# Gated linear attention and a channel mixer on one core: even-odd token order, column pieces of a weight, and a new issue order

## The chip, the core and the metric

The program runs on one core of a Trainium2 chip. The core has a matrix engine (TensorE, PE in the profile; its weight loads are PEld), VectorE (DVE), ScalarE (ACT), GpSimd (POOL) and SyncE (SP), which here only issues transfers. Sixteen DMA engines move data between HBM, the large memory, and SBUF, the memory on the chip; matmuls write into PSUM, eight banks of 2 KB per partition. The metric is the device time of one execution in microseconds (us), the median of several runs.

## The reference

Inputs are q, k, v and alpha of shape (4, 8, 768, 48), float32, and four weight matrices. First a recurrent attention for each batch and head, then a mixer over tokens and over channels:

```python
state = zeros(B, H, D, D)
for t in range(S):
    state = alpha[:, :, t, :, None] * state + einsum('bhd,bhe->bhde', k[:, :, t], v[:, :, t])
    y[:, :, t] = einsum('bhd,bhde->bhe', q[:, :, t], state)
x = y, as (B, 768, 384)
u = x + (relu(x^T @ w_tok1) @ w_tok2)^T          # w_tok1 768x256, w_tok2 256x768
out = u + relu(u @ w_ch1) @ w_ch2                # w_ch1 384x1536, w_ch2 1536x384
```

## The kernel before

The recurrence is computed in chunks of 256 tokens: three chunks per batch, n = 0 to 11. A partition of an input tile holds two neighbouring tokens (slots 0 and 1) of all 8 heads; the 128 partitions make two halves of 64, hf = 0 and 1, each with its own 128 tokens, and the state is carried from half to half. For one chunk the steps are: load alpha (`ld_at`), k, q, v; logarithms of alpha on ACT (`ln`, `lnP`); cumulative sums by a triangular matmul (`cum`, `cumw`); exponentials `E` and `IE` on ACT; k and q scaled by them (`kk`, `qq`); transposes of both. Chunks 0 to 5 transpose on TensorE into a PSUM bank (`trk`, `trq`), copied out by `evk` and `evq` into tiles tpk and tpq; chunks 6 to 11 transpose by a DMA issued on SP (`dk`, `dq`), and the query's result is copied once more (`pq`) into tpq. Then scores `G0`, `G1` for the two halves, a triangular mask on DVE (`mask`, tile gtm), the outer products `K`, the state updates `sa`, `sm`, `s`, the outputs `ia`, `ib`, `y`, and their copy to bf16 `x0`, `x1`.

The mixer of batch b takes the six x tiles of 128 tokens: `t1` (token matmul 1, six steps for each of two output blocks), `ht` (its relu), `t2` (token matmul 2) and `u` (the sum, on DVE). u is transposed to channels first: batch 0 on TensorE (`up`, `ut`), batches 1 to 3 by DMA on SP (`ux`). Then `c1`, 12 blocks of 128 channels for each half of the tokens, with relu `rt`; `c2`, 12 accumulating steps in four groups for each of six token tiles; the output sum `o` on DVE into one of three tiles o; and the store `st`, 192 KB, to HBM. The last batch's tile 0 is done in two half-wide parts (h0, h1).

Weights are loaded as 384 KB pieces into the pool of 19 input tiles (`ldw_`) and cast to bf16 (`cw_`): w_tok1 (wt1) and w_tok2 (wt2) in two pieces each, w_ch1 (wc1) and w_ch2 (wc2) in six each. In this kernel a piece of wc1 is 128 rows by 768 columns, so a `c1` block waits for three pieces.

The order of the work is written out: the text `ORDER` lists every operation in one sequence with a letter for its engine (t PE, s ACT, v DVE, g POOL, y SP), and `BUFS` the buffer of every tile. Each engine runs its operations in this order and waits at each for what it needs, so an operation that waits holds back all that follow on its engine. The entry `f8_trk0` and its like are fillers: matmuls on a zero tile ahead of the named operation, 8 units of 512 columns; every three units are issued as one float32 matmul (two rows in the profile), the rest as bf16. Operations on DVE and POOL that use the port which both share are also ordered one after another.

In the tiles tpq and tpk the 128 tokens of one half lie side by side. What comes from the transposes has the two slots apart, so the copies put them together. Before, the query copies place the two slots alternately, token by token:

```python
def qev(self, e, d, s):
    self.copy(e, self.t(d).rearrange("p (j c s) -> p s j c", j=4, s=2),
              s.rearrange("p (s j c) -> p s j c", s=2, j=4))
```

and the key copies place them as runs of 64 (slot 0, then slot 1, within each half).

Of the kernel before, what the change touches and what calls it, by code (L numbers as in the profile page):

```python
# [9 lines left out]
BF16 = mybir.dt.bfloat16  # L10
AF = mybir.ActivationFunctionType
ALU = mybir.AluOpType
# [89 lines left out]
UP = (0,)  # L102
# [11 lines left out]
SLOT = ()  # L114
# [6 lines left out]
def build(g):  # L121
# [18 lines left out]
    def attention(n):  # L140
# [64 lines left out]
        if n in KX:  # L205
            evk = O("dk", {"SP": (1240.0, 1240.0)}, 9, writes=[tpk], reads=[pkk], preds=kk,
                    emit=lambda e: g.xbar(tpk, pkk), dma=("x", 1400.0, 1180.0, 480.0))
            k_read = evk
        else:
            bk = V("one")  # L210
            k_read = O("trk", pe([128] * 8), 8, writes=[bk], reads=[pkk], preds=kk,
                       emit=lambda e: g.trw(bk, pkk))
            evk = O("evk", either(dve(1024, True), act(1024)), 9, writes=[tpk], reads=[bk], preds=[k_read],
                    emit=lambda e: g.trwev(e, tpk, bk, n not in SLOT))
        if n in QX:
# [3 lines left out]
            evq = O("pq", either(dve(1024), act(1024 * 1.35, True), {"POOL": (1100.0, 1140.0)}), 9.5, port=True, writes=[tpq], reads=[tqx], preds=[xq],  # L219
                    emit=lambda e: g.qev(e, tpq, g.t(tqx)))  # L220
        else:
# [3 lines left out]
            evq = O("evq", either(dve(1024 * 1.065), act(1024 * 1.34)), 9, writes=[tpq], reads=[bq], preds=[trq],  # L225
                    emit=lambda e: g.qev(e, tpq, g.bank(bq).bitcast(BF16)))
# [82 lines left out]
    def weight(nm, piece, prio, work=1100.0):  # L309
        raw = V("in")  # L310
        o = P.op(f"ldw_{nm}{piece}", LOADQ[0], prio, writes=[raw],
                 emit=lambda e: g.weight(e, nm, piece, raw, o), dma=("i", work, 1500.0, 650.0))
        wl[(nm, piece)] = P.op(f"cw_{nm}{piece}", either(dve(768, nm != "wc1"), pool_cp(768), act(768, True)), prio + 1,
                               reads=[raw], preds=[o], port=True, emit=lambda e: g.wcast(e, nm, piece, raw))

    def mixer(b):
# [16 lines left out]
        for i in range(NS):  # L333
            if i % 3 == 0:
# [3 lines left out]
                     reads=[h for h, _ in hts], preds=[h for _, h in hts] + [wl[("wt2", p)] for p in range(2)],  # L338
# [71 lines left out]
ld_at1y ld_at0y ln1s ln0s f8_cumw1t f1_cumw1t cumw1t IE1s cumw0t IE0s ld_vt0y E0s vb0g vs0_0g vs1_0v ld_kt0y kk0v  # L410
f8_trk0t f1_trk0t trk0t E1s ld_qt0y qq0v ka0s kb0s kc0v f1_trq0t trq0t ld_kt1y kk1v K0t evq0s s0_0v ld_vt1y vb1s
f1_trk1t trk1t ld_at2y evk0v ln2s f2_G0_0t G0_0t ld_qt1y ka1g sa1_0v f4_cumw2t cumw2t mask0_0v vs0_1s kb1g kc1g vs1_1s
K1t sm1_0g qq1v sa0_1v sm0_1v G1_0t ld_kt2y IE2s E2s trq1t evq1s ib0t mask1_0v f3_y1_0t y1_0t y0_0t evk1v G0_1t sa1_1v
ld_qt2y x1_0s mask0_1v G1_1t ld_vt2y x0_0s vb2s kk2g trk2t kc2s ldw_wt10y qq2g cw_wt10s f2_ia1t ia1t mask1_1v evk2s
trq2t ld_at3y vs1_2g ldw_wt11y evq2v ib1t y1_1t y0_1t vs0_2g ldw_wt21y sm1_1g P3g K2t sa0_2v sm0_2g x0_1s t1_0_0_0t
f1_G0_2t G0_2t ldw_wt20y G1_2t cw_wt20g t1_0_1_0t mask0_2v x1_1s t1_0_1_1t ld_at4y ld_kt3y t1_0_1_2t lnP3s cum3t
cw_wt11s IE3s ia2t y0_2t x0_2s t1_0_0_1t t1_0_0_2t E3s t1_0_0_3t mask1_2v t1_0_1_3t ib2t y1_2t ldw_wc14y t1_0_1_4t
x1_2s t1_0_0_4t f1_t1_0_1_5t t1_0_1_5t ht_0_1v P4g cw_wt21s t1_0_0_5t ht_0_0s f3_t2_0_0t t2_0_0t t2_0_1t u_0_0v ln13s
r13s ldw_wc13y t2_0_2t u_0_1v t2_0_3t u_0_2v t2_0_5t lnP4s t2_0_4t u_0_3v u_0_5v u_0_4v up_0_0t cw_wc14s cw_wc13s
ldw_wc15y up_0_1t ld_qt3y k0a3g kk3g cum4t trk3t cw_wc15g ut_0_0v up_0_2t ut_0_2v ut_0_1s c1_0_11_0t c1_0_8_0t IE4s  # L420
c1_0_11_1t rt_0_8_0v rt_0_11_0v ldw_wc11y q0r3g qq3g c1_0_9_1t rt_0_9_1v ln14s kb3s c1_0_10_0t cw_wc11s c1_0_9_0t
rt_0_9_0v rt_0_11_1v E4s c1_0_7_0t c1_0_10_1t c1_0_7_1t ldw_wc10y r14s cw_wc10s rt_0_10_1v trq3t evk3s rt_0_7_0v
ldw_wc12y ld_vt3y cw_wc12g c1_0_2_0t c1_0_0_1t ka3g rt_0_7_1s c1_0_8_1t rt_0_10_0v vb3v vs1_3g vs0_3g rt_0_0_1v
rt_0_2_0v evq3s ld_at5y ld_qt4y c1_0_1_1t rt_0_8_1v c1_0_3_0t kc3s K3t P5g c1_0_4_1t rt_0_3_0s rt_0_1_1s q0r4g G0_3t
ld_kt4y qq4g s0_3v ln15s G1_3t sa1_3v c1_0_2_1t rt_0_2_1s mask0_3v lnP5s c1_0_1_0t c1_0_5_1t rt_0_5_1s rt_0_1_0s r15s
mask1_3v ldw_wc21y cw_wc21s k0a4g ldw_wc20y c1_0_6_1t rt_0_6_1v c1_0_4_0t kk4v ldw_wc22y c1_0_5_0t c1_0_0_0t cw_wc22s
rt_0_4_0v rt_0_0_0v cw_wc20g rt_0_4_1s c1_0_6_0t rt_0_6_0v c1_0_3_1t trq4t rt_0_3_1v cum5t trk4t ld_kt5y k0a5g
ldw_wc23y rt_0_5_0s c2_0_3_0t c2_0_5_0t evq4s kb4s evk4v ld_qt5y G1_4t mask1_4v G0_4t ld_vt4y c2_0_0_0t IE5s c2_0_0_1t
ka4g cw_wc23s c2_0_3_1t kc4s sm1_3g E5s mask0_4v ib3t y1_3t ldw_wc24y cw_wc24s c2_0_5_1t vb4g vs1_4s x1_3s ia4t
ldw_wc25y vs0_4g cw_wc25s ld_at6y y0_3t kk5v c2_0_3_2t y0_4t q0r5v trk5t evk5s qq5v K4t c2_0_0_2t sa0_4v c2_0_0_3t P6v  # L430
x0_3s ld_at7y sm0_4g o_0_0v trq5t x0_4s sa1_4v P7g evq5s lnP6s c2_0_5_2t c2_0_5_3t ld_vt5y vb5g c2_0_4_0t c2_0_4_1t
ld_kt7y kc5g G1_5t G0_5t lnP7s o_0_5v ib4t y1_4t vs1_5s mask1_5v t1_1_1_0t t1_1_1_1t sm1_4g x1_4s c2_0_4_2t c2_0_3_3t
vs0_5s ld_at8y t1_1_1_2t st_0_5s K5t mask0_5v sa0_5v sm0_5v cum6t t1_1_0_0t ld_kt6y k0a6g t1_1_0_1t ld_qt6y c2_0_2_0t
ln17s ld_qt7y ia5t y0_5t x0_5s IE6s kk6g ib5t y1_5t ln16s E6s t1_1_0_2t x1_5v t1_1_0_3t t1_1_1_3t cum7t E7s o_0_3v
t1_1_1_4t t1_1_1_5t r16s ld_kt8y q0r6g ld_vt6y dk6y P8g ht_1_1v lnP8s t1_1_0_4t t1_1_0_5t c2_0_2_1t c2_0_2_2t ln18s
ht_1_0v t2_1_1t u_1_1v t2_1_2t t2_1_0t t2_1_4t u_1_2v u_1_0v ux_1_0y c2_0_1_0t c2_0_1_1t vb6s IE7s qq6v r17s t2_1_3t
u_1_3v c2_0_2_3t ka6s kc6s t2_1_5t o_0_2v u_1_4v c2_0_1_2t st_0_0y st_0_3s cum8t k0a8g c2_0_1_3t u_1_5v q0r7v vs1_6v
dq6y c2_0_4_3t c1_1_8_0t rt_1_8_0v IE8s c1_1_11_0t vs0_6s c1_1_5_0t E8s c1_1_10_0t o_0_4v c1_1_4_0t k0a7g ux_1_1y
o_0_1v kb6g rt_1_4_0v pq6s K6t s0_6v sa1_6v c1_1_3_0t rt_1_3_0v c1_1_0_0t rt_1_5_0s ld_at9y rt_1_0_0v rt_1_11_0s
c1_1_10_1t c1_1_2_0t c1_1_6_0t rt_1_6_0v r18s G0_6t G1_6t rt_1_10_0s rt_1_10_1s c1_1_1_0t qq7g rt_1_2_0s mask1_6v  # L440
c1_1_7_0t rt_1_7_0v ld_vt7y ld_qt8y c1_1_6_1t rt_1_6_1v c1_1_9_1t c1_1_11_1t kk7g ka7s vb7s c1_1_8_1t st_0_1s ld_at10y
kk8g rt_1_1_0s mask0_6v c1_1_3_1t ib6t rt_1_9_1v rt_1_3_1v c1_1_1_1t rt_1_8_1s P9g y0_6t vs1_7s x0_6v q0r8g c1_1_7_1t
qq8g rt_1_7_1v rt_1_11_1s y1_6t c1_1_5_1t rt_1_5_1v dk8y rt_1_1_1s vs0_7v dq7y kb7v sm1_6v c1_1_9_0t dk7y kc7g
c2_1_2_0t c1_1_2_1t rt_1_9_0v c1_1_0_1t lnP9s cum9t E9s x1_6v c2_1_2_1t c1_1_4_1t rt_1_4_1v pq7g K7t IE9s c2_1_2_2t
c2_1_2_3t sa0_7v rt_1_2_1s st_0_2y dq8y pq8g ld_vt8y G1_7t G0_7t mask1_7v ld_at11y sm0_7g sa1_7v ld_qt9y rt_1_0_1s
# [520 lines left out]
```

## Time and profile before

| | |
|---|---|
| timed runs | 163.34, 163.48, 164.39 us; median 163.48 |
| profiled execution | span of 160.5 us from the first to the last instruction; the profile gives no other time of it |
| median less span | 3.0 us |
| PE, PEld busy | 154.6 us (96%), 97.1 us (60%) |
| DVE, ACT, POOL busy | 114.9, 97.8, 80.8 us |
| DMA | 35.05 MB in 76,130 packets; 25.17 MB read from HBM, 4.72 MB written |

How to read what follows. A line of a group gives the source line, the engine, the operation, out<-in with the tiles' names, the shape and the count; after the first bar the time for which the group keeps its engine busy (us) and the mean duration of one (ns); after the second the time for which the engine sat idle just before them, and who ended that. A line of the timeline begins with start and duration in us; several equal instructions are merged (x7), and a bracket tells an idle time before it. A line of the stretches has the bounds, their length, and then busy us and instruction count of PE, PEld, DVE, ACT and POOL, the granted clock of TensorE, the mean busy share of the 16 DMA engines and the GB/s. The digits of the slices are tenths, forty slices to the span. The queue q1 is that of SP's transfers, q10 that of ACT's; a queue's line has packets, MB and share. The granted clock is 1.00 throughout.

### The profile page before, as it was taken

The page shows a single profiled execution, that of the slowest core. Times are in us where ns is not written, and L with a number is a line of the kernel's source. Part 1 is how long each engine was busy: PE and PEld are TensorE (multiplying, and loading weights), DVE is VectorE, ACT ScalarE, POOL GpSimd, SP SyncE. Part 2 cuts the span into 40 slices and gives each one's busy share as a digit, 9 for nine tenths or more (in the row PEclk, how much of TensorE's full clock was granted, in tenths as well). Part 3 has the DMA queues.
Part 4 walks back from the last instruction along what each step waited for, and adds up shares of the span by engine and source line. Part 5 has one row for each costly group of instructions (what it writes and reads, how often), then busy time and mean ns, then how long its engine had stood idle before and what let it go on. Part 6 is the DMA issues. An engine that isn't in the chain of part 4 may idle for free.

```text
span 160.5 us, 3971 instructions
## 1 busy us (share of the span) xinstructions
PE 154.6 (96%) x1563; PEld 97.1 (60%) x1563; DVE 114.9 (72%) x206; ACT 97.8 (61%) x179; POOL 80.8 (50%) x94
## 2 busy tenths in 40 slices
PE   7999989999999999999999999999999999999992
PEld 2545565766667676666667666566567665665661
DVE  6099994979889787989969758795886762464222
ACT  3789999998899955897563583269832203343000
POOL 5205897695973649389778852699523000000000
PEclk9999999999999999999999999999999999999999
DMA  4999999999999999999989999989701235111133
GB/s 122 320 324 317 317 374 311 339 333 306 316 347 324 275 278 272 210 228 319 241 202 298 239 315 204 217 196 134 196 21 62 87 79 169 49 49 53 49 129 116
DMA packets 76130, 35.05 MB, mean 218 GB/s; under 512 B 70352, under 2 KB 74320, under 8 KB 76112
## 3 DMA queue, kind: packets, MB, share of 16 engines
q1 hardware_dynamic: 73808, 31.76, 74.1%
q10 hardware_dynamic: 2304, 3.05, 5.3%
q8 instruction: 12, 0.20, 0.5%
q14 instruction: 6, 0.05, 0.1%
HBM read 25.17 MB, written 4.72 MB: 186 GB/s over the span
## 4 chain that ended last, share of the span: by engine, by line
PE 61%; DMA 12%; DVE 6%; ACT 6%; SPq 6%; POOL 4%; issue 3%; DVEq 0%; POOLq 0%
PE ps L907 22%; PE ps L902 21%; PE ps L643 11%; DMA in<-in_v_dram 6%; SPq L584 6%; DMA out_dram<-o 4%; PE ps L878 3%; PE ps L883 2%; DMA ut<-u 2%; DVE pkk L700 2%; DVE gtm L770 1%; PE ps L712 1%; DVE rt L875 1%; POOL vb L746 1%; POOL pkq L700 1%
## 5 line engine op out<-in xcount | busy, mean ns | idle before, releaser
L907 PE MATMUL ps<-wc,rt 128*128 128x384 bf16 (+1 forms) x300 | 52.4, 319 | 0.0
L902 PE MATMUL ps<-ut,wc 128*128 128x384 bf16 x288 | 50.3, 326 | 0.1
L902 PEld LDWEIGHTS <-wc 128*128 128x128 bf16 x288 | 27.1, 98 | 17.9 <-DMA ut<-u 0.6
L907 PEld LDWEIGHTS <-rt 128*128 128x128 bf16 x300 | 27.8, 98 | 16.0
L873 ACT ACTIVATE rt<-ps 128x384 bf16<-128x384 f32 x47 | 21.4, 492 | 23.6 <-PE ps L902 23.3
L875 DVE TENSOR_SCALAR rt<-ps 128x384 bf16<-128x384 f32 x49 | 25.6, 551 | 9.1 <-PE ps L902 8.9
L770 DVE TENSOR_TENSOR gtm<-ps,mk 128x1024 bf16<-128x1024 f32 x24 | 28.5, 1218 | 3.1 <-PE ps L643 2.8
L911 DVE TENSOR_TENSOR o<-ps,u 128x384 f32<-128x384 f32 (+1 forms) x25 | 13.2, 536 | 12.6 <-PE ps L907 10.1
L700 POOL TENSOR_TENSOR pkk<-in,IE 128x768 bf16<-128x768 f32 x8 | 14.5, 1817 | 3.3 <-DVE ss L844 2.3
L745 ACT CAST x<-ps 128x384 bf16<-128x384 f32 x20 | 9.2, 479 | 11.1 <-PE ps L643 9.5
L887 DVE TENSOR_TENSOR u<-ps,x 128x384 bf16<-128x384 f32 x24 | 12.0, 550 | 3.1 <-PE ps L883 2.5
L746 POOL CAST vb<-in 64x384 bf16<-64x384 f32 (+1 forms) x14 | 8.3, 594 | 10.4 <-DMA in<-in_v_dram 4.7
L692 POOL TENSOR_TENSOR in<-in,in 128x384 f32<-128x384 f32 x8 | 8.0, 1000 | 10.5 <-DVE u L887 3.8
L643 PE MATMUL ps<-rt 128*128 128x512 bf16 (+1 forms) x29 | 12.1, 515 | 1.1 <-DVE rt L541 1.1
L745 ACT CAST vb<-in 64x384 bf16<-64x384 f32 (+1 forms) x18 | 11.4, 634 | 0.8 <-DMA in<-in_v_dram 0.3
L700 POOL TENSOR_TENSOR pkq<-in,E 128x768 bf16<-128x768 f32 x6 | 10.9, 1818 | 0.6 <-DMA tpk<-pkq 0.3
L878 PE MATMUL ps<-x,wt 128*128 128x384 bf16 x48 | 11.0, 325 | 0.0
L844 POOL TENSOR_TENSOR ss<-tmp,E 128x384 bf16<-128x384 f32 x10 | 8.3, 833 | 4.2 <-DVE in L628 3.9
L841 DVE TENSOR_TENSOR tmp<-ps,ss 128x384 f32<-128x384 f32 x16 | 8.8, 552 | 1.8 <-PE ps L643 0.6
L883 PE MATMUL ps<-ht,wt 128*128 128x384 bf16 x48 | 9.1, 326 | 0.0
L643 PE MATMUL ps<-vb,gtm 128*128 128x48 bf16 x192 | 8.2, 183 | 0.2 <-DVE gtm L770 0.2
L643 PE MATMUL ps<-tpq,tpk 48*64 48x128 bf16 (+1 forms) x288 | 7.9, 218 | 0.4 <-POOL tpq L746 0.3
(94 smaller groups left out, 207.6 us busy)
## 6 DMA issues: line engine op xcount, KB each, us to landing
in<-in_alpha_dram SPq DMA_DIRECT2D x12, 384.0 KB, 5.1
in<-in_v_dram SPq DMA_DIRECT2D x12, 384.0 KB, 5.6
in<-in_k_dram SPq DMA_DIRECT2D x12, 384.0 KB, 5.2
in<-in_q_dram SPq DMA_DIRECT2D x12, 384.0 KB, 5.5
in<-in_moe_w_ch_dram SPq DMA_DIRECT2D x12, 384.0 KB, 5.9
out_dram<-o ACTq DMA_DIRECT2D x15, 192.0 KB, 1.8
in<-in_moe_w_tok_dram SPq DMA_DIRECT2D x4, 384.0 KB, 6.0
out_dram<-o SPq DMA_DIRECT2D x8, 192.0 KB, 2.2
```

Of the source, the lines that this page charges most:

```text
L643: return self.pe.matmul(out, lhsT=lhsT, rhs=rhs, start=start, stop=stop, skip_group_check=True)
L700: self.shared(self.eng[e].tensor_tensor(self.t(dst)[:, :, h0:h1, 0:D], self.t(src)[:, h0:h1].rearrange("p h s d -> p s h d"), bass.AP(tens ...
L745: return self.act.copy(d, s)
L770: self.nc.vector.tensor_tensor(self.t(gtm)[:, hf, :, :], self.pair(gp).rearrange("p a (j t) -> p (a j) t", t=128), bass.AP(tensor=m.tensor ...
L873: self.act.activation(d, s, AF.Relu)
L875: self.nc.vector.tensor_scalar_max(d, s, 0.0)
L878: self.pe.matmul(self.bank(bank)[:, 0:HD], lhsT=self.wt1[:, kc, m * 128 : m * 128 + 128], rhs=self.t(x), start=(kc == 0), stop=(kc == NS - 1))
L883: self.pe.matmul(self.bank(bank)[:, 0:HD], lhsT=self.wt2[:, kc, i * 128 : i * 128 + 128], rhs=self.t(hts[kc]), start=(kc == 0), stop=(kc = ...
L887: self.nc.vector.tensor_tensor(self.t(u)[:, i % 3], self.bank(bank)[:, 0:HD], self.t(x), ALU.add)
L902: self.pe.matmul(self.bank(bank)[:, 0:HD], lhsT=self.wc1[:, kc, mc * 128 : mc * 128 + 128], rhs=self.t(ut)[:, 3 * half : 3 * half + 3, kc, ...
L907: self.pe.matmul(self.bank(bank)[:, 0 : cz - ca], lhsT=self.t(rts[mc][0])[:, i * 128 : i * 128 + 128], rhs=self.wc2[:, mc, ca:cz], start=( ...
L911: self.nc.vector.tensor_tensor(self.t(o)[:, ca:cz], self.bank(bank)[:, 0 : cz - ca], self.t(u)[:, i % 3, ca:cz], ALU.add)
```

## The change

Five things are edited together.

1. All query copies (`evq`, `pq`) use the layout that the key copies have: runs of 64, so that within a half the even tokens come first and then the odd ones. The masks, the token weights and the stores follow: row p of an x, u or o tile is now an even token for p < 64, an odd one from 64 on.
2. `wt1` is loaded as even rows into partitions 0 to 63 and odd rows into 64 to 127, two transfers a piece (`a`, `b`). The cast of `wt2` puts its columns into even-odd order; its two pieces are now halves of the columns.
3. `wc1` is loaded in six column pieces of 256, all 384 rows of them; a `c1` block waits for the one piece with its columns, a `t2` block for one piece of wt2.
4. The mask constants are made by copies of the triangular tiles on DVE, and no longer by POOL.
5. `ORDER` and `BUFS` are new throughout: the engine of many operations, the places of all of them, and the fillers.

```diff
-            evq = O("evq", either(dve(1024 * 1.065), act(1024 * 1.34)), 9, ... emit=lambda e: g.qev(e, tpq, g.bank(bq).bitcast(BF16)))
+            evq = O("evq", either(dve(1024, True), act(1024)), 9, ... emit=lambda e: g.merged(e, tpq, g.bank(bq).bitcast(BF16)))
...
+    def merged(self, e, d, s):
+        self.copy(e, self.t(d).rearrange("p (g s t) -> p s g t", g=8, s=2), s.rearrange("p (s g t) -> p s g t", s=2, g=8))
...
         if nm == "wt1":
-            w = self.w[0].rearrange("(c p) m -> p c m", p=128)
-            self.gated(dma(t.rearrange("p (c m) -> p c m", c=3), w[:, 3 * piece : 3 * piece + 3, :]), op)
+            w = self.w[0].rearrange("(c p s) m -> s p c m", p=64, s=2)[part]
+            self.gated(dma(t[64 * part : 64 * part + 64].rearrange("p (c m) -> p c m", c=3), w[:, 3 * piece : 3 * piece + 3, :]), op)
...
-            c, h = piece % 3, piece // 3
-            self.gated(dma(t, self.w[2][128 * c : 128 * c + 128, 768 * h : 768 * h + 768]), op)
+            w = self.w[2].rearrange("(c p) m -> p c m", p=128)
+            self.gated(dma(t.rearrange("p (c m) -> p c m", c=3), w[:, :, 256 * piece : 256 * piece + 256]), op)
...
+    def rows(self, d):
+        return d.rearrange("(p s) c -> s p c", s=2)
+
     def store(self, e, o, b, i, ca, cz):
-        self.queue(e).dma_start(self.out[b, i * 128 : (i + 1) * 128, ca:cz], self.t(o)[:, ca:cz])
+        self.queue(e).dma_start(self.rows(self.out[b, i * 128 : (i + 1) * 128, ca:cz]), self.t(o)[:, ca:cz])
...
-                     ... preds=[h for _, h in hts] + [wl[("wt2", p)] for p in range(2)],
+                     ... preds=[h for _, h in hts] + [wl[("wt2", i // 3)]],
...
-    ... [wl[("wc1", p)] for p in ((0, 1, 2) if mc < 6 else (3, 4, 5))],
+    ... [wl[("wc1", mc // 2)]],
...
 ORDER (first lines)
-ld_at1y ld_at0y ln1s ln0s f8_cumw1t f1_cumw1t cumw1t IE1s cumw0t IE0s ld_vt0y E0s vb0g vs0_0g vs1_0v ld_kt0y kk0v
-f8_trk0t f1_trk0t trk0t E1s ld_qt0y qq0v ka0s kb0s kc0v f1_trq0t trq0t ld_kt1y kk1v K0t evq0s s0_0v ld_vt1y vb1s
+ld_at0y ld_at1y ln0s f12_cumw0t f4_cumw0t cumw0t ln1s ld_kt0y cumw1t IE0s kk0v f2_trk0t trk0t ld_qt0y E0s qq0v trq0t
+evk0v evq0v f3_G1_0t G1_0t mask1_0v E1s IE1s ld_qt1y qq1g trq1t G0_0t ka0s kb0s ld_vt0y vb0s vs1_0s vs0_0s kc0g K0t
...
 ORDER (last lines)
-c2_3_3_2t c2_3_3_3t c2_3_4_0t o_3_3v st_3_3y c2_3_4_1t c2_3_4_2t c2_3_4_3t o_3_4v c2_3_1_1t c2_3_1_2t c2_3_1_3t o_3_1v
-st_3_4s c2_3_0h0_0t c2_3_0h0_1t c2_3_0h0_2t c2_3_0h0_3t o_3_0h0v st_3_0h0y st_3_1s
+st_3_0h0s c2_3_1_1t c2_3_1_2t c2_3_1_3t c2_3_2_0t o_3_1v st_3_1s c2_3_4_3t c2_3_2_1t c2_3_2_2t o_3_4v st_3_4s
+c2_3_5_0t c2_3_5_1t c2_3_2_3t o_3_2v st_3_2s c2_3_5_2t c2_3_5_3t o_3_5v st_3_5y c2_3_0h1_2t c2_3_0h1_3t o_3_0h1v
+st_3_0h1s
```

In the new order the loads begin at0, at1, kt0, qt0, qt1, vt0, kt1, at2, vt1, kt2, vt2, qt2 (before: at1, at0, vt0, kt0, qt0, kt1, vt1, at2, qt1, kt2, qt2, vt2). Of the 25 stores 19 are issued on ACT and 6 on SP (before 16 and 9). The copies `evq` of chunks 0, 2, 3 and 4 stand on DVE and two on ACT (before one on DVE, five on ACT); of the six `pq` four stand on ACT, one on DVE, one on POOL (before two on ACT, four on POOL).

More of the change, by code (lines that the diff above doesn't have):

```diff
@@ L213, in attention @@
             evk = O("evk", either(dve(1024, True), act(1024)), 9, writes=[tpk], reads=[bk], preds=[k_read],
-                    emit=lambda e: g.trwev(e, tpk, bk, n not in SLOT))
+                    emit=lambda e: g.merged(e, tpk, g.bank(bk).bitcast(BF16)))
         if n in QX:
@@ L545, in __init__ @@
         make_identity(nc, self.idn)
-        gp.memset(self.mk, 1.0)
-        gp.memset(mkb, 1.0)
-        for t, base in ((self.mk, 0), (mkb, 127)):
-            gp.affine_select(out=t, in_=t, compare_op=ALU.is_ge, fill=0.0, base=base,
-                             pattern=[[1, 128]], channel_multiplier=-2)
         dv.memset(self.sel, 0.0)
```

203 lines of the change are left out of this document (98 added, 105 removed), and 22 rows, old and new, of the table BUFS.

## The prediction

> **What bounds the kernel now.** I read the page first (busy shares, slices, queues), then the groups by form, the start-up in the timeline, and the stretches after the first store.
>
> ```profile
> span 160.5 us, 3971 instructions
> PE 154.6 (96%) x1563; PEld 97.1 (60%) x1563; DVE 114.9 (72%) x206; ACT 97.8 (61%) x179; POOL 80.8 (50%) x94
> DMA  4999999999999999999989999989701235111133
> q10 hardware_dynamic: 2304, 3.05, 5.3%
> HBM read 25.17 MB, written 4.72 MB: 186 GB/s over the span
> ...
> L643 PE MATMUL ps<-rt 128*64 128x384 f32 x14 | 6.9, 607 | 1.1 <-DVE rt L541 1.1
> L643 PE MATMUL ps<-rt 128*128 128x512 bf16 x15 | 5.4, 429 | 0.0
> ```
>
> TensorE is busy for 154.6 of 160.5 us, and 6.9 + 5.4 = 12.3 us of that are filler matmuls on a zero tile, all in the start-up. So TensorE sets the end once its real work flows, and before that the chain of loads and evacuations does. The second resource that is full is the DMA engines: nines from the second slice to about two thirds of the span.
>
> ```profile
> 1.06 4.21 PE L643 MATMUL ps<-rt 128*64 128x384 f32 x7 [1.06 <-DVE rt L541]
> 3.88 0.19 DVE L569 COPY mk<-rt 64x128 bf16<-64x128 bf16 x1
> 5.17 0.71 PE L643 MATMUL ps<-la,u 128*128 128x384 bf16 x3
> 6.32 0.81 ACT L687 ACTIVATE IE<-ps 128x768 f32<-128x768 f32 x1
> 6.37 0.65 PE L643 MATMUL ps<-la,u 128*128 128x384 bf16 x3
> 7.34 2.26 PE L643 MATMUL ps<-rt 128*64 128x384 f32 x7
> 7.45 0.81 ACT L687 ACTIVATE IE<-ps 128x768 f32<-128x768 f32 x1 [0.32 <-PE ps L643]
> 8.33 0.35 DVE L746 CAST vb<-in 64x384 bf16<-64x384 f32 x1 [4.26 <-POOL vb L746]
> 19.34 0.83 ACT L745 CAST vb<-in 128x768 bf16<-128x768 f32 x1
> 20.49 0.62 PE L712 MATMUL ps<-idn,pkq 128*128 128x128 bf16 x8
> 22.52 0.53 DVE L841 TENSOR_TENSOR tmp<-ps,ss 128x384 f32<-128x384 f32 x1
> 23.17 2.36 DVE L770 TENSOR_TENSOR gtm<-ps,mk 128x1024 bf16<-128x1024 f32 x2
> 31.76 1.46 PE L902 MATMUL ps<-ut,wc 128*128 128x384 bf16 x8
> ```
>
> The start-up ends at 31.76, where the long run of channel matmuls begins. The twelfth attention load is there at 19.34; the last masks of chunk 2 end at 25.53.
>
> **The change, part by part.** The sum is made against the span of 160.5; the median of the runs, 163.48, lies 3.0 above it, and I carry that.
>
> *Query evacuations.* The six query copies from PSUM and the six from SBUF now use the layout that the key copies have already.
>
> ```profile
> L745 ACT COPY tpq<-ps 128x1024 bf16<-128x1024 bf16 x5 | 6.6, 1320 | 0.5 <-PE ps L712 0.5
> L745 ACT COPY tpk<-ps 128x1024 bf16<-128x1024 bf16 x3 | 3.0, 1010 | 0.0
> L746 DVE COPY tpk<-ps 128x1024 bf16<-128x1024 bf16 x3 | 2.0, 679 | 0.0
> L746 POOL COPY tpq<-tpk 128x1024 bf16<-128x1024 bf16 x4 | 5.3, 1335 | 1.9 <-PE ps L902 1.8
> L745 ACT COPY tpq<-tpk 128x1024 bf16<-128x1024 bf16 x2 | 2.7, 1338 | 0.0
> L700 POOL TENSOR_TENSOR pkq<-in,E 128x768 bf16<-128x768 f32 x6 | 10.9, 1818 | 0.6 <-DMA tpk<-pkq 0.3
> L700 DVE TENSOR_TENSOR pkq<-in,E 128x768 bf16<-128x768 f32 x6 | 5.7, 955 | 0.3 <-POOL in L628 0.2
> ```
>
> From PSUM, ACT goes from 1320 to 1010 ns, DVE to 679. From SBUF the new layout is not shown: between 1010 and 1338 on ACT, up to 1335 on POOL; I take 1010 and 1335. In all the side engines shed some 5 us, which TensorE at 96% hides. It counts only in chunk 2, on the start-up's chain. There the new order puts the query scaling on DVE (955) where before it was on POOL (1818), and the copy on DVE (679). But the query load is now the twelfth: 19.35 + 0.95 scaling + 0.67 transposes + 0.68 copy + 0.55 state add + 0.5 scores and hops = 22.7, then 2.36 of masks: 25.05, against 25.53. DVE is full up to there, so 0.5 us is all I take, and it arrives at 31.76 as 31.3.
>
> *Fillers.* Sorted by form, the f32 rows go from 14 to 12 and the bf16 rows from 15 to 10, 2.8 us by their groups. That is no gain by itself, since they stand in waits. But the first group grows from 9 units to 16. The same seven instructions take 4.21 us at the start and 2.26 later, so the array runs at half speed up to about 5.2. Sixteen units then end near 5.2 + 7 x 0.22 = 6.7, not 5.17, and the first cumulative matmuls wait behind them: IE of chunk 0 starts at 7.8, where before the first one started at 6.32 and this one at 7.45. Late next is the chunk-0 key scaling; chunk 2 waits for its load until 19.35 anyhow, which absorbs most. I take +0.2, and up to +1.4 if none is absorbed. The Trainium skill, "TensorE: Matmul & The Clock Gate", Part 1, says that the clock opens after about 3.4 us of sustained work in a free-running window; the 4.1 us here agree, and by it the gate could open as late as 7.9 in some runs, which would make this term 1 us larger.
>
> *Weights.* The token weights come as four loads of 64 partitions in place of two; wc1 in six column pieces with 1 KB runs in place of 3 KB, so a channel matmul waits for one piece, not three.
>
> ```profile
> 21.70:22.60 0.90, 0.87 (x19) 0.51 (x16) 0.90 (x2) 0.90 (x2) 0.90 (x2) 1.00 1.05 405
> 27.00:30.00 3.00, 3.00 (x18) 1.46 (x18) 2.17 (x5) 2.97 (x7) 2.73 (x2) 1.00 1.03 333
> 8.00:12.00 4.00, 3.73 (x35) 1.84 (x33) 3.58 (x6) 3.48 (x6) 0.30 (x2) 1.00 1.17 324
> ```
>
> In the last two columns (DMA share, GB/s) the stretch with 1 KB runs (first row) is no slower than the one with 3 KB (second), so 0; the bound is the 384-byte loads (third), 17% more share per byte, 1 us of transfers over six pieces, under cover of TensorE's work in hand. A half load could cost as much as a whole one: two extra loads of 1.2 us before 31.76, at most +1.1 there. The finer waits gain nothing at 31.76, which is set by u and its transposes. Half-row token order leaves the number and shape of matmuls and masks alone: 0. The constants take six more small DVE copies (the one of 64x128 above took 0.19) after 3.9, done by 5.5, before DVE's first work on data at 8.33: 0.
>
> *Stores.* This is the term that decides. The tile's rows are now even tokens, then odd ones, so the store writes to HBM with a pattern of 2 x 64 x 384 (the built program says so) where it was 128 x 384. Look at q10: 16 stores made 2304 packets, 144 each: 128 rows and 16 more. So a store is cut into sixteen shares, each closing with a packet of its own, and every transfer of this trace has 128 rows as its first dimension. If shares are cut along the first dimension, the new store can be cut into two at most, and two engines of the sixteen carry it all.
>
> By the Trainium skill, "DMA: Bandwidth & Descriptors", section "Why a DMA increments its semaphore by 16 and not by 1", that is so: the number of engines is the largest up to 16 that divides the slowest dimension on both sides, here 2. No run here shows it yet.
>
> ```profile
> 56.70:60.00 3.30, 3.30 (x48) 2.32 (x45) 3.00 (x4) 1.66 (x4) 1.11 (x3) 1.00 1.03 289
> 60.00:80.00 20.00, 20.00 (x193) 12.59 (x192) 17.70 (x33) 14.99 (x31) 16.22 (x13) 1.00 1.06 254
> 80.00:100.00 20.00, 20.00 (x241) 13.07 (x240) 15.41 (x26) 11.10 (x24) 13.02 (x14) 1.00 0.99 253
> 100.00:120.00 20.00, 19.64 (x242) 12.39 (x241) 15.63 (x23) 12.41 (x24) 13.32 (x13) 1.00 0.75 156
> 120.00:140.00 20.00, 20.00 (x158) 12.54 (x156) 11.09 (x22) 4.41 (x10) 1.46 (x3) 1.00 0.30 89
> 140.00:160.50 20.50, 17.41 (x119) 11.10 (x117) 7.47 (x15) 3.84 (x9) 0.00 (x0) 1.00 0.21 78
> ...
> L624 ACTq DMA_DIRECT2D out_dram<-o x16: 338/338/390, 56.9 to 157.0; - x16
> DMA to landing us min/median/max: 1.6/2.0/5.8
> ```
>
> In these rows, too, the last two columns are DMA share and GB/s. The last stretch, nearly all stores, moves 78 GB/s at 0.21 of sixteen engines: 23.2 GB/s for each busy one. 4.72 MB of stores cost each of sixteen engines 12.7 us, but each of two 101.7 us; one 192 KB store takes 4.24 us there. The first store is issued at 56.9, and in the new order after 588 matmuls (before: 591), so about the same time. From then on an engine has 3.4 + 21.2 + 19.8 + 15.0 + 6.0 + 4.3 = 69.7 us of packets (share x stretch), 57.0 without stores. On the two engines that becomes 57.0 + 101.7 = 158.7. Packets overlap up to a share of 1.17 (the 384-byte row above): between 135.6 and 158.7 us of time; I take 1.06, at which these loads ran: 149.7. Every load and every DMA transpose needs all its engines, so the two slow ones delay them all. TensorE waits at the transposes of u ahead of each channel stage, and DVE at the output adds, for only three output tiles exist, and all of DVE queues behind such a wait. So the ledger of the two engines is the bound: 56.9 - 0.3 + 149.7 + 2.2 (what follows a last transfer: 160.5 less the last add's end at 157.8, less 0.5 of transfer) = 208.5, plus 3.0: 211.5.
>
> ```profile
> 133.97 10.72 PE ps L902 x66
> 157.44 0.36 DVE o L911
> ```
>
> **Rivals.** *Only the tail pays* (earlier loads and stores fit into slack). The last seven stores follow the first of them by only 45 matmuls, 39 of 162 ns (10.72/66) and 6 half ones, 6.8 us. The first of them is ready near 157.4 - 6.8 - 0.3 + 0.7 = 151.0; 5 x 4.24 + 2 x 2.12 = 25.4 us on two engines and 2.2 give 178.6, plus 3.0: 181.6 (177.9 at 1.17). Against it: shares of 1.06 and 0.99 from 60 to 100 leave no slack for ten stores.
> *The store stays in sixteen shares* (the queue cuts by rows, whatever the pattern). Then -0.3 at the start, +0.2 at the end, since two output adds follow each other there: 163.4, 161 to 165. Against: nothing in the trace has rows grouped in this way. This is the case on the other side, decided by whether a store still closes with sixteen packets.
> *Sixteen shares, but a late start*: the filler's 1.4 and the half loads' 1.1 are not absorbed: 166.
>
> **How the numbers follow.** Two engines with the full ledger 0.66; tail alone 0.17; sixteen shares 0.11; sixteen and late 0.06. I lean to two shares because the one fact the trace has on cutting, sixteen closings for 128 rows, fits a cut along the first dimension, and the edit changes that dimension. Range: 177 (the tail at 1.17) to 224 (56.9 + 158.7 + 2.2 + 3.0 = 220.8, and some us for idle engines and a cold array after long waits). Faster by over 1% is 0.06 and within 1% 0.05 out of the third case, to which the fourth adds 0.02 within 1%; the rest, 0.87, is slower (1%, 1.6 us, is about what a measurement of this kernel can tell from no change).
>
> **What would show it.** Right: 130 packets per store on q10 where 144 were; landing of stores at 4 us and more by the median (now 2.0); output adds and TensorE's weight loads of the channel stage waiting for DMA; TensorE's share near 75%; the last store ending over 10 us after the last matmul. The start-up: channel matmuls from 31 to 32, query copies of 680 on DVE and 1010 on ACT, first cumulative matmul near 6.7. Wrong: 144 packets per store, and landings near 2.

## The result, and the profile after

The changed kernel took 222.94 us (median of 4 runs, 221.04 to 225.05), the kernel before, run beside it, 163.41: a ratio of 1.360, 95% interval 1.348 to 1.371. This ratio, like those below, is of the fast runs alone, and of the four runs the one of 225.05 us, which is also the profiled one, counts as slow. The forecast was 211.5 us in a range of 177 to 224: slower, by the term named, but 11.4 us short. The profiled execution has a span of 223.2 (the other three 219.2 to 222.5), where the forecast's sum gave 208.5. Its added 3.0 for the time outside the span was too much: in every run of the record the time is 1.7 to 1.9 above the span.

The page of the changed kernel: span, engines, slices, the two queues and the chain that ended last.

```profile
span 223.2 us, 3968 instructions
PE 164.4 (74%) x1556; PEld 99.6 (45%) x1556; DVE 114.7 (51%) x206; ACT 102.4 (46%) x194; POOL 70.5 (32%) x79
PEclk9999999999996959995599985999999889997555
DMA  6999999999973889989994938972317410101111
...
q10 hardware_dynamic: 2470, 3.54, 4.6%
HBM read 25.17 MB, written 4.72 MB: 134 GB/s over the span
...
DMA 43%; PE 35%; SPq 10%; DVE 5%; issue 2%; ACT 1%; ACTq 0%; DVEq 0%
```

q10 is the first thing to read. Its 19 stores made 2470 packets, 130 each: 128 rows and two closings (the packet that ends a share), where before there were 128 and sixteen. Both kernels move 25.17 and 4.72 MB, so nothing more is transferred; a store is only spread over fewer engines. TensorE has fallen to 74% of the span, and the chain is now led by DMA. Its busy time has grown too (154.6 before), though there are no more matmuls (1556, before 1563): the slices of granted clock fall to 5 and 6 in and behind the waits.

Three stretches of the windows (PE, PEld, DVE, ACT, POOL busy with counts, clock, DMA share, GB/s), pieces of the chain (start, length, link), and the waits of the output adds and the channel stage.

```profile
57.00:80.00 23.00, 13.78 (x124) 8.18 (x117) 8.70 (x14) 9.74 (x21) 7.17 (x9) 0.87 0.70 167
100.00:120.00 20.00, 11.90 (x184) 8.09 (x185) 8.77 (x13) 8.11 (x14) 2.89 (x5) 0.74 1.11 178
200.00:223.20 23.20, 1.90 (x15) 1.15 (x13) 1.94 (x4) 0.00 (x0) 0.00 (x0) 0.58 0.13 47
...
58.10 8.45 DMA out_dram<-o
72.62 7.90 DMA ut<-u
94.07 13.99 DMA tpk<-pkk
113.09 7.92 DMA out_dram<-o
125.50 9.05 DMA ut<-u
...
DVE o L905 <- DMA out_dram<-o: 29.0, 7, 6.9
PE ps L896 <- DMA ut<-u: 14.6, 3, 6.0
```

The first store is issued at 58.10, and from there the chain alternates: an output add waits for a store to give its tile back, then TensorE waits for the transposes of u or of a key chunk. At the end the store traffic is alone:

```profile
204.54 0.56 DVE L905 TENSOR_TENSOR o<-ps,u 128x384 f32<-128x384 f32 x1 [6.93 <-DMA out_dram<-o]
208.46 1.02 DVE L905 TENSOR_TENSOR o<-ps,u 128x384 f32<-128x384 f32 x2 [3.36 <-DMA out_dram<-o]
212.39 0.36 DVE L905 TENSOR_TENSOR o<-ps,u 128x192 f32<-128x192 f32 x1 [2.90 <-DMA out_dram<-o]
```

The tiles come back 3.92 and 3.93 us apart (204.54, 208.46, 212.39): one 192 KB store after the other. The forecast's 4.24 at its overlap of 1.06 is 4.00, so here its price holds. The DMA share from 200 on fits as well: 0.13 of sixteen engines are two.

### The profile page after: what moved, and what is told of

It is laid out like the page before. It is cut to its first block, busy times and chain, and to the rows that moved or that the text cites. A ratio compares the mean times of both kernels' runs of the same rounds, so it can differ in the third digit from the quotient of the medians.

```text
span 223.2 us, 3968 instructions
## 1 busy us (share of the span) xinstructions
PE 164.4 (74%) x1556; PEld 99.6 (45%) x1556; DVE 114.7 (51%) x206; ACT 102.4 (46%) x194; POOL 70.5 (32%) x79
## 3 DMA queue, kind: packets, MB, share of 16 engines
q10 hardware_dynamic: 2470, 3.54, 4.6%
HBM read 25.17 MB, written 4.72 MB: 134 GB/s over the span
## 4 chain that ended last, share of the span: by engine, by line
DMA 43%; PE 35%; SPq 10%; DVE 5%; issue 2%; ACT 1%; ACTq 0%; DVEq 0%
PE ps L896 19%; DMA out_dram<-o 17%; DMA ut<-u 10%; DMA tpk<-pkk 9%; PE ps L901 8%; SPq L582 6%; DMA in<-in_moe_w_ch_dram 3%; PE ps L645 3%; DMA in<-in_alpha_dram 3%; PE ps L877 2%; DVE o L905 2%; SPq L598 2%; SPq L601 1%; PE ps L872 1%; DVE gtm L764 1%
## 5 line engine op out<-in xcount | busy, mean ns | idle before, releaser
L896 PE MATMUL ps<-ut,wc 128*128 128x384 bf16 x288 | 56.0, 351 | 16.3 <-DMA ut<-u 14.6
L901 PE MATMUL ps<-wc,rt 128*128 128x384 bf16 (+1 forms) x300 | 55.3, 327 | 0.8 <-ACT rt L867 0.8
L896 PEld LDWEIGHTS <-wc 128*128 128x128 bf16 x288 | 29.3, 104 | 39.3 <-DMA ut<-u 12.8
L867 ACT ACTIVATE rt<-ps 128x384 bf16<-128x384 f32 x59 | 27.0, 490 | 34.6 <-PE ps L896 34.2
L869 DVE TENSOR_SCALAR rt<-ps 128x384 bf16<-128x384 f32 x37 | 19.9, 554 | 23.3 <-PE ps L896 20.3
L905 DVE TENSOR_TENSOR o<-ps,u 128x384 f32<-128x384 f32 (+1 forms) x25 | 13.2, 539 | 34.2 <-DMA out_dram<-o 29.0
L838 POOL TENSOR_TENSOR ss<-tmp,E 128x384 bf16<-128x384 f32 x13 | 10.9, 836 | 28.6 <-DVE tmp L835 28.6
L740 ACT CAST vb<-in 64x384 bf16<-64x384 f32 (+1 forms) x25 | 15.0, 598 | 5.6 <-DMA in<-in_v_dram 3.8
L645 PEld LDWEIGHTS <-tpk 48*64 48x64 bf16 (+1 forms) x288 | 6.2, 108 | 13.0 <-DMA tpk<-pkk 9.1
L702 DVE TENSOR_TENSOR pkk<-in,IE 128x768 bf16<-128x768 f32 x5 | 4.8, 958 | 13.0 <-POOL in L698 6.5
L645 PE MATMUL ps<-rt 128*64 128x384 f32 (+1 forms) x22 | 9.8, 567 | 1.0 <-DVE rt L544 1.0
```

Of the source, the lines that this page charges most:

```text
L645: return self.pe.matmul(out, lhsT=lhsT, rhs=rhs, start=start, stop=stop, skip_group_check=True)
L702: self.shared(self.eng[e].tensor_tensor(self.t(dst)[:, :, h0:h1, 0:D], self.t(src)[:, h0:h1].rearrange("p h s d -> p s h d"), bass.AP(tens ...
L740: return self.act.copy(d, s)
L867: self.act.activation(d, s, AF.Relu)
L869: self.nc.vector.tensor_scalar_max(d, s, 0.0)
L896: self.pe.matmul(self.bank(bank)[:, 0:HD], lhsT=self.wc1[:, kc, mc * 128 : mc * 128 + 128], rhs=self.t(ut)[:, 3 * half : 3 * half + 3, kc, ...
```

## The experiments

Two theories stood against each other: the two engines that carry each store (A), and the rest of the change: order, layout, weights (B). Times are medians; each ratio is to the kernel before, run beside it on the same chip (162.49, 162.37 and 162.82 us).

### The store alone, from both sides

e1_split, in the changed kernel:

```diff
-        self.queue(e).dma_start(self.rows(self.out[...]), self.t(o)[:, ca:cz])
+        for s in range(2):
+            self.queue(e).dma_start(self.rows(self.out[...])[s], self.t(o)[64 * s : 64 * s + 64, ca:cz])
```

> The changed kernel with one thing altered: each output store goes out as two DMAs of 64 rows (even tokens, then odd), each with 64 as its first dimension, instead of one of 2 x 64. The rest of the change stays (new layout, plain query copies, weights in pieces, new issue order). Theory A, two engines of sixteen carry every 2 x 64 x 384 store: with 64 rows every store is again spread over sixteen engines, the whole loss goes, and the time is 163.4 (161 to 166), with the same 26.4 us shares of DMA and no wait of VectorE for an output store of more than 2 us. q10 shows 64 + 16 = 80 packets for each half, 160 a store. Rival B, the new issue order or the new layout itself costs the time: it stays above 200. Rival C, half and half: 175 to 195.

Measured: 170.82 us, ratio 1.050 (1.044 to 1.056). On q10 a half has 80 packets (3040 for 38), 64 rows and sixteen closings. So 52.1 of the 59.5 us go with this one line; theory A holds for the bulk and B falls. The halves write the same rows to the same places in HBM as the single store did, so it is not the alternating rows that cost the time. But 163.4 was expected, so 7 to 8 us remained to be explained.

e2_first2, e3_first4 and e4_first8, the kernel before with another first dimension (2, 4 or 8 for k):

```diff
-        self.queue(e).dma_start(self.out[...], self.t(o)[:, ca:cz])
+        d = self.out[...].rearrange("(p s) c -> s p c", s=k)
+        self.queue(e).dma_start(d, self.t(o)[:, ca:cz])
```

> The kernel before with one thing altered: the output side of each store is written as 2 x 64 x 384 (row 2p+s of a tile to slot s, p), so rows land in another order within each tile of 128; nothing of the changed kernel's order, layout or weights is in it. Theory A (two engines carry it): the ledger of the prediction for this order, 56.9 + 149.7 + 2.2 + 3.0 = 211.8, or, as the changed kernel came out 11 us above it, up to 223; so 205 to 225, and q10 at 130 packets a store. Rival B (order, layout): 163 to 166.

> The kernel before with the output side of each store written as 4 x 32 x 384 (rows land in another order within a tile). Theory A, as many engines as the first dimension has: four engines carry the stores, 50.9 us on each of four beside 57.0 of other packets, 107.9 / 1.06 = 101.8 of time from 56.9: 56.9 + 101.8 + 2.2 + 3.0 = 163.9 by the ledger alone, and with the last stores slower (2.1 us of transfers each, two on a queue at the end: +2) 164 to 172; 132 packets a store. Rival, a store is cut in two or sixteen whatever the first dimension: 205 to 225 or 163.

> The kernel before with the output side of each store written as 8 x 16 x 384 (rows land in another order within a tile). Theory A: eight engines, 25.4 + 57.0 = 82.4 us of packets on each, under TensorE's 96 to 100 us that are left: 163.5 to 165, 136 packets a store. Rival, a first dimension that is split into any number of parts costs the same: 205 to 225.

Measured: 230.01 (ratio 1.412, 1.403 to 1.420), 191.83 (1.177, 1.169 to 1.184) and 173.09 (1.065, 1.060 to 1.070). The packets of q10 in these three pages, 16 stores each, and VectorE's wait for output tiles:

```profile
q10 hardware_dynamic: 2080, 3.05, 4.1%
DVE o L912 <- DMA out_dram<-o: 47.4, 13, 7.8
```
```profile
q10 hardware_dynamic: 2112, 3.05, 5.3%
DVE o L912 <- DMA out_dram<-o: 20.2, 10, 4.7
```
```profile
q10 hardware_dynamic: 2176, 3.05, 6.5%
DVE o L912 <- DMA out_dram<-o: 9.4, 5, 3.0
```

130, 132 and 136 packets a store: 2, 4 and 8 closings. The number of shares is the first dimension of the pattern, and the store by itself, put into the old order, costs as much as the whole change. The Trainium skill, "DMA: Bandwidth & Descriptors", section "Why a DMA increments its semaphore by 16 and not by 1", gives the number of engines as the largest up to 16 that divides the slowest dimension on both sides; the counts of all four forms (130, 132, 136 and 144) agree with it.

The times for four and eight were missed by 20 and 8 us, both too low. The ledger of the forecast takes a row at its price in sixteen shares; either that price or the ledger was wrong. e12_stages below bears on it.

### What is left when the store is whole again

e5_plain: the changed kernel with `self.out[b, i * 128 : (i + 1) * 128, ca:cz]` as the store's target in place of `self.rows(...)` of it.

> The changed kernel with one thing altered: each store writes its 128 rows to 128 rows in a row (128 x 384), one DMA as in the kernel before, so tokens land in another order within a tile of 128; everything else of the change stays. Theory A, what is left of the loss with two half stores (170.8 against 162.5) is the price of the second DMA (50 issues of 0.58 us in place of 25, and the half behind it): it goes, 162 to 165, the forecast's own case of sixteen shares (163.4). Rival B, the new order costs it (the first channel matmul at 32.2 in place of 31.8, a wait of 4.5 us for the transposes of u at 65.9, one of 1.5 us near 92): 167 to 171.

Measured: 165.23 us, ratio 1.018 (1.015 to 1.021). So the second DMA of e1_split was 5.6 us, and 2.9 were left that are not stores. 165.23 lies 0.2 above theory A's range and below B's. The channel matmuls wait 0.5 us in all for the transposes of u (2.6 in e1_split), so that part of B falls; the first channel matmul stood at 32.81, even later than B's 32.2.

e6_split_f9: e1_split with a shorter filler group.

```diff
-ld_at0y ld_at1y ln0s f12_cumw0t f4_cumw0t cumw0t ...
+ld_at0y ld_at1y ln0s f8_cumw0t f1_cumw0t cumw0t ...
```

> The changed kernel with half stores as in e1_split, and the filler group ahead of the first cumulative matmul cut from 16 units (f12, f4) to 9 (f8, f1), as many as the kernel before had. The prediction's term: 7 cold units of 0.22 us, so the first cumulative matmul at about 5.2 in place of 6.6 to 7.0; +0.2 of the time if the loads absorb it, up to +1.4 if not: e1_split less 0.2 to 1.4, 169.4 to 170.6. Rival: the array is then cold for the work behind it and nothing is won, 170.8 or more.

Measured: 171.45 us, ratio 1.055 (1.051 to 1.059): no gain. The first cumulative matmuls and a later one (chunk 4), of e1_split and then of e6_split_f9:

```profile
6.61 0.65 PE L646 MATMUL ps<-la,u 128*128 128x384 bf16 x3
31.41 0.32 PE L646 MATMUL ps<-la,u 128*128 128x384 bf16 x1
```
```profile
5.13 0.65 PE L646 MATMUL ps<-la,u 128*128 128x384 bf16 x3 [0.43 <-ACT la L640]
31.49 0.32 PE L646 MATMUL ps<-la,u 128*128 128x384 bf16 x1
```

In these two profiles the seven units more hold the first chunk up by 1.48 us, and by 31 us nothing of it is left. With the long filler group this matmul stands at 6.18 (e5_plain), 6.61, 6.70 (e11_plain_wt1) and 7.01 (the changed kernel), so the 1.48 are 1.0 to 1.9. What absorbs them was not isolated; the forecast named the loads.

e11_plain_wt1: e5_plain with whole loads of wt1. Two of the four entries for these loads also go from `ORDER`, and the second piece is loaded where its first half stood.

```diff
-        for z in range(2 if nm == "wt1" else 1):
+        for z in range(1):
...
-            w = self.w[0].rearrange("(c p s) m -> s p c m", p=64, s=2)[part]
-            self.gated(dma(t[64 * part : 64 * part + 64].rearrange(...), w[:, 3 * piece : 3 * piece + 3, :]), op)
+            w = self.w[0].rearrange("(c p) m -> p c m", p=128)
+            self.gated(dma(t.rearrange(...), w[:, 3 * piece : 3 * piece + 3, :]), op)
```

> The changed kernel with plain stores as in e5_plain, and the token weights wt1 loaded as two whole loads of 128 partitions in place of four halves (weight rows then stand in plain order: the tokens get each other's weights; the work is the same). In e5_plain the first channel matmul stood at 32.8 against 31.8 before. Theory, the half loads are the prediction's term of 0 to 1.1: the first channel matmul comes to 31.8 to 32.3 and the time is 164.2 to 164.9. Rival, what is late there is the cast of wt2 on POOL behind it or the third chunk's state: 32.8 stays and so do 165.2.

Measured: 162.95 us, ratio 1.001 (0.998 to 1.005), so 2.3 us less than e5_plain and the time of the kernel before; it is 1.2 below what was expected. First channel matmul and the next attention load on SP's queue, of e5_plain and of e11_plain_wt1:

```profile
32.81 3.41 PE L896 MATMUL ps<-ut,wc 128*128 128x384 bf16 x20
23.37 0.47 SPq L582 DMA_DIRECT2D in<-in_alpha_dram  x1
57.00:80.00 23.00, 22.04 (x179) 13.56 (x178) 15.76 (x28) 15.62 (x35) 12.04 (x13) 1.00 1.06 269
80.00:100.00 20.00, 18.80 (x275) 12.45 (x273) 16.22 (x25) 13.40 (x27) 11.62 (x14) 1.00 1.15 255
```
```profile
31.81 4.38 PE L896 MATMUL ps<-ut,wc 128*128 128x384 bf16 x26
21.31 0.47 SPq L582 DMA_DIRECT2D in<-in_alpha_dram  x1
57.00:80.00 23.00, 22.45 (x188) 13.93 (x186) 15.83 (x29) 15.61 (x35) 12.93 (x14) 1.00 1.11 268
80.00:100.00 20.00, 19.36 (x272) 12.65 (x270) 17.12 (x26) 14.06 (x27) 12.05 (x14) 1.00 0.98 246
```

The two extra loads hold up everything behind them on SP's queue, here by 2.06 us (23.37 against 21.31). These are single profiles: e1_split and e6_split_f9 have the extra loads too, and there this load stands at 22.30 and 22.60 and the first channel matmul at 32.17 and 32.23. One us shows here at the first channel matmul, and a second one from 57 to 100, where TensorE is idle for 2.16 us (0.96 + 1.20) in the one and 1.19 (0.55 + 0.64) in the other. With stores and wt1 whole, all the rest of the change (query copies, layout, column pieces, fillers, order) is together worth nothing that can be measured; parts of it may offset each other.

### The second DMA of a store

e9_split_2q: e1_split with `self.nc.sync` as the queue of the second half in the last batch.

> The changed kernel with half stores as in e1_split, and for the last batch the second half of every tile issued by SP's queue in place of the first half's. In e1_split VectorE waited 4.2 us for output stores, most of it among the last four tiles, and the last matmul ended 5.0 before the end (3.1 in the kernel before). Theory: the second issue of 0.58 us and the half behind it are what is late there, so the tail shrinks by 1 to 2: 169 to 170. Rival, the half stores cost their price in the body (transposes of u waited for at 65.9) and the tail is hidden: 170.8.

Measured: 170.43 us, ratio 1.045 (1.040 to 1.050), within the interval of e1_split. The second queue at the end wins nothing that can be told, though VectorE waits only 1.1 us for output tiles (4.2 in e1_split).

e10_before_split: the kernel before, each store as two DMAs of 64 rows.

> The kernel before with each store as two DMAs of 64 rows in a row (same rows, same places), nothing else. Theory A: the price of a second DMA for each store is that of e1_split over e5_plain, 5.6 us, in any order: 167 to 169. Rival B: it is the new order that has no room for it; here it is the issue of the second half at the end alone, 163 to 165.

Measured: 167.62 us, ratio 1.028 (1.022 to 1.034): 4.8 us, near the 5.6 in the new order, so theory A: the second DMA has its price in either order. The issues of the stores on ACT's queue, of e10_before_split (minimum, median, maximum in ns):

```profile
L625 ACTq DMA_DIRECT2D out_dram<-o x32: 473/580/1515, 56.7 to 161.0; - x32
```

Each half takes longer to issue (580 ns) than the whole store did (338), on ACT, which stands between TensorE's stages. How the 5 us divide into these issues and the later landing was not tried.

### Body and tail

e7_tail2 and e8_body2: e1_split's two halves where `b < B - 1` (e7) or `b == B - 1` (e8), the changed kernel's single DMA elsewhere.

> The changed kernel with stores of 2 x 64 x 384 in one DMA only for the last batch (seven stores, six stores' bytes); the stores of batches 0 to 2 go as two halves of 64 rows. By the transfers alone: the last batch's outputs leave from about 153, six times 4.1 us of transfers is 24.6, so the last one lands near 178 and the run takes 178 to 184 (the prediction's rival of a tail alone: 181.6, 177.9 at the least), 8 to 13 above e1_split. Rival: the tail hides behind the last channel stage as before: 171 to 173.

> The reverse: 2 x 64 x 384 stores for batches 0 to 2, halves for the last batch. If the two engines' packets alone set the time (the prediction's ledger): 57.0 + 18 x 4.24 = 133.3 on each, / 1.06 = 125.8, so 58 + 125.8 + 5.2 = 189. If every late store and every late transpose is waited for in turn, and TensorE slows down in the waits (theory of the chain): the 223 of the changed kernel less its tail of 26 - 5 = 21 us: about 202.

Measured: 187.83 us (ratio 1.153, 1.147 to 1.159) and 203.65 (1.254, 1.249 to 1.260). Over e1_split that is 17.0 for the tail and 32.8 for the body, together 49.8 of 52.1: the two add up nearly. The tail of e7_tail2:

```profile
156.79 17.60 ACTq L630 DMA_DIRECT2D out_dram<-o  x6
165.66 0.56 DVE L909 TENSOR_TENSOR o<-ps,u 128x384 f32<-128x384 f32 x1 [6.95 <-DMA out_dram<-o]
```

From the first issue (156.79) to the end of the span (184.2) it takes 27.4 us; the forecast's rival had 25.4 + 2.2 = 27.6, but from 151.0; this kernel also carries the halves and the loads of e1_split, 8.3 us over the kernel before. The body is where the ledger with the forecast's price failed (189 expected, 203.65 measured).

### The price of a store by itself

e12_stages leaves out the computation and issues transfers alone, with VectorE's memset of the tile as the next writer.

> Transfers by themselves, one stage after the other, the computation left out: a 192 KB store of one output tile with 128, 2, 4 and 8 as its first dimension; two of them at a time on two queues; two halves; a DMA transpose of u and a 384 KB load, alone and behind a store of 128, 2 or 8. Theory (shares by the first dimension, 65 ns for a row, some 1.1 us around): 1.6, 5.3, 3.2 and 2.1 us from issue to the next writer of the tile; two at a time on the same two engines 9.5, on different ones 5.3; and if all shares of a transpose or a load must end, behind a store of 2 it takes some 4 us longer than alone, not 4 us only when queues are served in turn. As the runs with 4 and 8 came out longer than the ledger: if a lone store of 4 takes 4.0 and of 8 takes 2.7, the rows are slower by themselves; if 3.2 and 2.1, what makes them slow is the traffic beside them.

The stages of the first 45 us ran into each other and aren't used for prices. The later stores stand alone. VectorE's row is the memset that waited; the store goes out 0.41 us after its start:

```profile
45.76 0.38 DVE L52 MEMSET o<- 128x384 f32 x1 [0.22 <-DMA out_dram<-o]
46.17 15.36 ACTq L65 DMA_DIRECT2D out_dram<-o  x4
48.28 0.38 DVE L52 MEMSET o<- 128x384 f32 x1 [2.14 <-DMA out_dram<-o]
55.23 0.38 DVE L52 MEMSET o<- 128x384 f32 x1 [5.76 <-DMA out_dram<-o]
60.50 0.38 DVE L52 MEMSET o<- 128x384 f32 x1 [4.89 <-DMA out_dram<-o]
64.39 0.38 DVE L52 MEMSET o<- 128x384 f32 x1 [3.51 <-DMA out_dram<-o]
67.82 0.38 DVE L52 MEMSET o<- 128x384 f32 x1 [3.05 <-DMA out_dram<-o]
```

The four stores are those of 128, 2, 4 and 8. From issue to the next writer they take 2.11, 6.54, 4.86 and 3.48 us (48.28 - 46.17; 55.23 - 48.69; 60.50 - 55.64; 64.39 - 60.91), and two halves 3.02; for four and eight that is above even the 4.0 and 2.7 that were named for slower rows. Later stores of 128, 2 and 8 in the same trace repeat this (2.09, 6.57 and 6.53, 3.50 and 3.47).

How much of it is the transfer can be read from the DMA share between the first and the last packet of a store, here of 128 (the later one), 2, 4 and 8:

```profile
72.62:73.29 0.67, 0.00 (x0) 0.00 (x0) 1.00 0.81 291
49.88:54.70 4.82, 0.00 (x0) 0.00 (x0) 1.00 0.13 41
56.85:59.96 3.11, 0.00 (x0) 0.00 (x0) 1.00 0.23 63
62.17:63.82 1.65, 0.00 (x0) 0.00 (x0) 1.00 0.45 119
```

(Bounds, length, DVE, POOL, clock, DMA share, GB/s.) Length x share x 16, over the engines that carry the store, makes 0.54, 5.0, 2.9 and 1.5 us of packets on each engine. By rows, of which an engine has 8, 64, 32 and 16, that is 68, 78, 89 and 93 ns, where rows of 66 ns would make 4.22, 2.11 and 1.06 us in the last three. The first packet also comes later, 1.19 to 1.26 us after the issue in place of 0.84. So the rows of a lone store are slower in two, four or eight shares than in sixteen, with no traffic beside it. Why is open, and it is not so everywhere: back to back in the tail of the changed kernel a store takes 3.92 us, 61 ns for a row.

With this price the ledger of the forecast can be done over, (57.0 + 24 stores) / 1.06: 56.9 + 167.0 + 5.2 = 229.1 for two engines in the old order (230.01 measured), but 56.9 + 119.4 + 5.2 = 181.5 for four (191.83), and from 58.1 it gives 230.3 for the changed kernel (222.94). For eight the engines come to 149.8, under TensorE's bound, and 173.09 was measured. So the price alone does not explain the times. The ledger also has its engines never idle, and they are: e3_first4 moves nothing from 136.25 to 141.65, and e2_first2 nothing from 151.80 to 156.50, while TensorE is busy throughout. For eight VectorE waits 9.4 us for output tiles, and how that becomes 10 us was not taken apart.

## Why the prediction was right, and where it fell short

*Two engines carry every store*: right. 130 packets where 130 were named, and first dimensions of 2, 4, 8 and 128 make 2, 4, 8 and 16 closings.

*What this costs*: the cause was right, and the sum came out short in two places. The first is its step "the ledger of the two engines is the bound", which never lets them rest between the first store and the last. The forecast had idle engines only as a reserve in its range. In two stretches of the changed kernel no packet is in flight:

```profile
150.75:154.65 3.90, 2.68 (x45) 1.62 (x45) 2.03 (x4) 2.46 (x5) 2.98 (x2) 1.00 0.00 0
185.20:190.45 5.25, 5.25 (x37) 3.36 (x36) 2.53 (x5) 2.83 (x6) 0.00 (x0) 1.00 0.00 0
```

The DMA share is 0.00 in both, and in two shorter ones (155.80 to 156.45 and 195.32 to 196.85), 11.3 us in all; in the second row TensorE works the whole time, in the channel stages of the last batch, and the next store is issued only at 189.29. So the bound changes hands: the engines, then TensorE, on which the chain runs from 176.14 to 195.10, then the engines again. From the first store at 58.10 (56.6 forecast) to the end it is 165.1 us; the forecast had 149.7 + 2.2 = 151.9, and without the idle stretches 153.8 are left. That the two engines of the stores are busy in all of these 153.8 is not shown, since the trace does not name a packet's engine.

The second is the price of a store. The forecast divided the stretch at the old kernel's end, sixteen shares, by its busy engines and got 4.24 us. The line of q10 measures it in the kernel itself: 4.6% of sixteen engines over 223.2 us, for 17 whole stores and two half-wide ones, is 4.56 us of packets on each of two engines, 0.32 more than forecast, and 24 times that is 7.7 us. Read in the same way (15 whole stores and a half-wide one) e2_first2 has 4.81, e3_first4 2.60 and e4_first8 1.43, where 4.24, 2.12 and 1.06 were taken. Idle stretches and price make 19.0 us, more than the 13.2 by which the stretch was short, so another part of the ledger came out smaller, perhaps the overlap of 1.06; the runs do not separate them. That 229.1 comes near the 230.01 of e2_first2 proves neither.

*Late next*: the output adds and the transposes of u wait, as forecast; the DMA transposes of the key chunks (13.99 us at one place of the chain) it had only in the words that every DMA transpose is delayed. The clock of the array was only named as a reserve in the range: the same 1556 matmuls took 164.4 us of TensorE against 153.0 in e5_plain.

```profile
PE 153.0 (94%) x1556; PEld 96.6 (59%) x1556; DVE 114.3 (70%) x206; ACT 102.0 (62%) x194; POOL 70.4 (43%) x79
```

These 11.4 us are not the 11.4 by which the forecast was short. TensorE is not the bound in most of the changed kernel, so they lie partly under the waits; how much of them reaches the end was not measured.

*TensorE at 75%* (74), *the last store over 10 us after the last matmul* (issued at 212.8, the last matmul ended near 202; its landing is some 20 us after), *TensorE's weight loads waiting* (12.8 us for the transposes of u): right. *Landing at 4 us and more by the median*: the profile gives no landing of the changed kernel's stores; a lone one took 6.54 us until the tile could be written again.

*The start-up*: wrong. Channel matmuls came at 32.99 in place of 31 to 32. The copies are as short as forecast (680 and 1010; groups by form below: 692 from PSUM on DVE, 1048 from SBUF on ACT), but the 0.5 us of them did not arrive. The half loads were taken at 0 with a bound of 1.1; in the profiles that have them the first channel matmul comes 0.4 to 1.2 us later than the 31.81 of e11_plain_wt1, near the bound, and they cost 2.3 in the whole run, because the forecast looked only as far as 31.76 and not at the loads behind them on SP's queue. The filler's +0.2 is 0 within the measurement (first cumulative matmul at 6.18 to 7.01, 6.7 forecast). That the array starts at half speed shows only in the durations (4.21 against 2.26 us); the clock column of the kernel before reads 1.00 from 0 to 5.20, too.

```profile
L741 DVE COPY tpq<-ps 128x1024 bf16<-128x1024 bf16 x4 | 2.8, 692 | 0.4 <-PE ps L714 0.2
L740 ACT COPY tpq<-tpk 128x1024 bf16<-128x1024 bf16 x4 | 4.2, 1048 | 8.3 <-DMA tpk<-pkq 8.1
```

*Column pieces, finer waits, constants, layout: 0*: right together, by e11_plain_wt1 (1.001, 0.998 to 1.005).

*The rivals*: the tail alone (181.6) falls, since the body costs 32.8 by e8_body2. Its tail was about as long as forecast (27.4 us from the first issue), but begins at 156.79 in e7_tail2, not at 151.0. Sixteen shares (163.4) gives 165.23 in e5_plain and 162.95 without the half loads, so of the late start only these loads counted.

## What to carry to other kernels

Read a store's DRAM pattern as a share count: before a layout is changed so that rows interleave, count the closings per DMA in the queue's packets, and keep a first dimension that gives sixteen shares, as 64 and 128 did here (2, 4 and 8 gave only as many as they count). Splitting such a store in two is the cheap repair, but a second DMA for each store cost 5 us here, and two more loads early in a queue cost what they add to every later load on it, not only at the next wait. Price a resource at the width at which it will run (a store took 4.56 us of packets in two shares, not the 4.24 worked out from sixteen), and ask when it will have nothing to do: a sum over the busy time of one resource leaves out the stretches in which another holds it up.

## What the runs showed that I had not expected

In fewer shares than sixteen a lone store's rows are slower, and most in eight: 5.0, 2.9 and 1.5 us of packets in place of 4.22, 2.11 and 1.06 for two, four and eight (78, 89 and 93 ns for a row, 68 in sixteen).

Issuing depends on the pattern. A store of 128 x 384 took 338 ns on ACT's queue by the median, one of 2 x 64 x 384 took 522, of 4 x 32 x 384 547, of 8 x 16 x 384 614, and a half store 580. The row of the changed kernel:

```profile
L626 ACTq DMA_DIRECT2D out_dram<-o x19: 521/522/1122, 58.1 to 212.8; - x19
```

Slow stores hold up the issue of other transfers: the transposes of u, on SP's queue, took 3204 ns to issue by the median in the changed kernel and 1288 in e5_plain, whose stores alone differ.

```profile
L724 SPq DMA_TRANSPOSE ut<-u x6: 1277/3204/5624, 72.6 to 171.9; - x6
```
```profile
L724 SPq DMA_TRANSPOSE ut<-u x6: 1282/1288/1774, 65.3 to 134.4; - x6
```
